# Inducing-point attention and a gated feed-forward on one core: gates and side work share a ring of double PSUM banks, one running maximum a batch, stage 2 by pairs

## The chip, the cores and the metric

The kernel runs on one core of a Trainium2 chip. The metric is the time of one execution in microseconds (us) of device time; less is better. PE is TensorE (matmuls), DVE VectorE, ACT ScalarE, POOL GpSimd, SP the SyncE that issues most DMAs.

## The reference

Two layers, one behind the other. The attention has 4 batches of 12416 tokens with 128 channels and 32 inducing points:

```python
def mab(q, kv):
    s = scale * (q @ kv.transpose(0, 2, 1))
    s = s - s.max(-1, keepdims=True)
    a = np.exp(s)
    a /= a.sum(-1, keepdims=True) + 1e-09
    return a @ kv
h = mab(I, x)
return mab(x, h).astype(np.float32)
```

Its output (49664 tokens of 128) goes through the feed-forward, with 1536 hidden units:

```python
gate = 1.0 / (1.0 + np.exp(-(x @ w_gate)))
val = x @ w_val
return (gate * val @ w_out).astype(np.float32)
```

## The kernel before

**Stages.** A batch has 97 chunks of 128 tokens: six groups of 16 chunks and one lone chunk. Stage 1 (`mab(I, x)`) makes scores of the 32 inducing points against a group, takes a maximum of the group (`s1_max`, L202, DVE, from PSUM), an exponential with it as bias (`s1_exp`, L215, ACT), turns the weights round (by a transposing DMA, L239, or on PE for the lone chunk), and sums weights times x (`s1_sum_pe`, L250). `plan_combine` brings the groups of a batch, each with a maximum of its own, to one (POOL, L370 and the tree behind it), divides, and multiplies h into the gate and value weights: `hw` holds h times the weights, 32 rows for each. So a hidden unit of the feed-forward is a product over 32 inducing points, not over 128 channels. Stage 2 (`mab(x, h)`) makes the 32 scores of each token (`s2_score`, L418), copies them out of PSUM (`s2_take`, L455, ACT), finds the maximum of each token and takes it away on POOL (`s2_lower_pool`, L457), exponential on ACT (L479), sum, reciprocal and normalised weights on POOL (`s2_sum_pool`, `s2_inverse_pool`, `s2_spread`), and a transposing DMA on SP's queue (`s2_turn_dma`). The result is `a2`.

**The feed-forward** runs over 97 blocks of 512 tokens. A block has 12 hidden tiles of 128 units, worked in steps of two tiles and one tile in turn. For a step t PE fills a value bank and a gate bank (`hidden_mm`, L791, K = 32, in row groups of their own), ACT takes the gate's tanh (L809), and DVE makes u = (tanh + 1) x value (L818). PE projects u with `w_out` into `acc` (`project`, L847: four matmuls a tile), and ACT copies a finished block out, halved (L865).

**PSUM** has eight banks: gates two (double tiles) and one (single), values the same (`g2`, `g1`, `v2`, `v1`, each one buffer), `acc` one, and `m` one for all side work, that is all of stages 1 and 2 beside the feed-forward.

**Order.** Each engine runs its queue in the order in which the program names its instructions. In step t: value fill of t, gate fill of t + 2, product of t, tanh of t + 2, then side work due in this slot (`plan`, `at`; a slot is two steps), then up to three or four tiles of projection. A double product waits for the gate fill of t + 2. Stages 1 of the next batch and 2 of this and the next are laid into slots by hand, at the end of the function (L872 to L904).

**Start.** Stage 1 of batch 0, stage 2 of its first group, and the weights come before the first block, with the same functions and an order of their own; maxima of the last groups are joined at the end (`join_min`).

Of the kernel before, what the change touches and what calls it, by code (L numbers as in the profile page):

```python
# [17 lines left out]
P = 128  # L18
# [7 lines left out]
def kernel(  # L26
# [29 lines left out]
    s1p = ctx.enter_context(tc.tile_pool(name="s1p", bufs=4))  # L56
# [12 lines left out]


    xn, xT = {}, {}

    def x_load(b, s, first=0):
        c0, n = groups[s]
        if s == 0:
            c0, n = 0, n + NLO
        if b not in xn:
            xn[b] = xnp.tile([P, NCH, C], F16, tag="xn", name=f"xn_{b}")
        cuts = [c0, c0 + first, c0 + n] if first else [c0, c0 + n]
        for c, e in zip(cuts, cuts[1:]):  # L80
            nc.gpsimd.dma_start(xn[b][:, c:e, :], xv[b, :, c:e, :])
# [5 lines left out]
    def x_transpose_dma(b, s):  # L87
        c0, n = groups[s]
        xT_tile(b)
        nc.sync.dma_start(  # L90
            xT[b][:, c0 : c0 + n, :],
            xn[b][:, c0 : c0 + n, :].rearrange("p j c -> p (j c)"),
            transpose=True,
        )
# [38 lines left out]
    one1 = const.tile([1, 1], F32, tag="one1")  # L133
    nc.vector.memset(one1[:], 1.0)
    tiny = const.tile([P, 1], F32, tag="tiny")
    nc.vector.memset(tiny[:], TINY)
    minus1 = const.tile([P, GC + NLO], F32, tag="minus1")
# [9 lines left out]
    nm1s = [const.tile([P, NS], F32, name=f"nm1_{q}", tag=f"nm1_{q}") for q in range(2)]  # L147
    l1s = const.tile([P, NS], F32, name="l1_0", tag="l1_0")
    hsts = [const.tile([P, NS, C + 1], F32, name=f"hst_{q}", tag=f"hst_{q}") for q in range(2)]
    nc.vector.memset(l1s[:], 0.0)  # L150
    for q in range(2):
        nc.vector.memset(nm1s[q][:], NEG)
        nc.vector.memset(hsts[q][:, at_col[NG], :], 0.0)

    indT = const.tile([P, m], F16, tag="indT")
    indT_ps = ps.tile([P, m], F32, tag="m", name="indT_ps")
    nc.tensor.matmul(indT_ps[:], ind32[:], identf[0:m, 0:m], start=True, stop=True)
    nc.vector.tensor_scalar_mul(out=indT[:], in0=indT_ps[:], scalar1=SCALE)
# [3 lines left out]
    summed = [0] * B  # L162
    def s1_sum(b, s, a1, tag):
        hp = ps.tile([P, C + 1], F32, tag=tag, name="hp_ps")
        s1_sum_pe(b, s, a1, hp, 0, 4)
        return s1_sum_keep(b, s, hp)

    plan = {}

    def at(slot, make, late=False):  # L170
        plan.setdefault((slot, late), []).append(make)


    def s1_col(b, s):
        p = at_col[s]
        if b == 0 and p >= EARLY:
            return nml, l1l, slice(1 + p - EARLY, 2 + p - EARLY)
        return nm1s[b % 2], None if b else l1s, slice(p, p + 1)
# [6 lines left out]
    def s1_score_pe(b, s, tag):  # L185
        c0, n = groups[s]
        ng, w, R = s1_dims(s)
        s1 = ps.tile([P, 512], F32, tag=tag, name="s1_ps")
        for g in range(ng):
            nc.tensor.matmul(  # L190
                s1[32 * g : 32 * g + 32, 0 : w * P],
# [4 lines left out]
            )  # L196
        return s1

    def s1_max(b, s, s1):
        ng, w, R = s1_dims(s)  # L200
        nm, _, col = s1_col(b, s)
# [4 lines left out]
    def s1_score(b, s, tag):  # L206
        s1 = s1_score_pe(b, s, tag)
        s1_max(b, s, s1)
        return s1

    def s1_exp(b, s, s1):
        ng, w, R = s1_dims(s)
        nm, l1, col = s1_col(b, s)
        a1T = s1p.tile([P, 512], F16, tag="a1T")
        nc.scalar.activation(  # L215
            out=a1T[0:R, 0 : w * P],
# [3 lines left out]
            **({} if b else dict(accum_out=l1[0:R, col])),  # L220
# [3 lines left out]
    def s1_turn_pe(b, s, a1T, tag="m"):  # L224
        ng, w, R = s1_dims(s)
        aT = ps.tile([P, 4, P], F16, tag=tag, name="aT_ps")
        for k in range(w):
            nc.tensor.transpose(aT[:, k, 0:R], a1T[0:R, ts(k, P)], ident[0:R, 0:R])  # L228
        return aT

    def s1_turn_copy(s, aT):
        ng, w, R = s1_dims(s)
        a1 = s1p.tile([P, 4, P], F16, tag="a1")
# [3 lines left out]
    def s1_turn_dma(b, s, a1T):  # L237
        a1 = s1p.tile([P, 4, P], F16, tag="a1")
        nc.sync.dma_start(a1[:], a1T[:], transpose=True)  # L239
        return a1  # L240

    def s1_sum_pe(b, s, a1, hp, k0, k1):
        c0, n = groups[s]
        ng, w, R = s1_dims(s)
        for k in range(k0, min(k1, w)):
            for cols, src in ((slice(0, C), None), (slice(C, C + 1), ones16[:])):
                for g in range(ng):
                    if b == 0 and src is not None:
                        continue
                    nc.tensor.matmul(  # L250
                        hp[32 * g : 32 * g + 32, cols],
                        a1[:, k, 32 * g : 32 * g + 32],
                        xn[b][:, c0 + g * w + k, :] if src is None else src,
                        start=(k == 0 and src is None),
                        stop=(k == w - 1),
                        skip_group_check=True,
                    )

    def s1_sum_keep(b, s, hp):
        ng, w, R = s1_dims(s)  # L260
        width = C + 1 if b else C
        summed[b] += 1
        if b == 0 and at_col[s] > EARLY:
            return hp[:, 0:C]
# [696 lines left out]
```

## Time and profile before

| | |
|---|---|
| time, median of 3 runs | 730.15 us (730.0 to 739.06) |
| span of the profiled execution, first to last instruction | 728.4 us |
| TensorE clock granted, mean | 0.988 |
| first product of the feed-forward | 33 us into the span |
| products (L818) | 388 of 1024 elements, 387 of 512, 2 of 256 |

The time of the profiled execution is not listed by itself. Busy time is the union of an engine's records; where neighbouring records overlap, a group's count times its mean is more than its busy time. A group's line gives: line of the kernel, engine, operation, output and inputs by the program's names with their shapes, count, busy time in us, mean duration in ns, then idle time of the engine just before them and what ended it. "DVE busy in stages": from 100 to 700 us it is 99.9% or more of every 100 us, ScalarE 95 to 97%, TensorE 90 to 91%, GpSimd 43 to 74%. The DMA engines are 89% busy from 40 to 100 us, then half or less. A timeline line gives the start in us, the length in us of what was merged, engine, line, operation, and how many.

### The profile page before, as it was taken

What the parts mean: (1) busy time and instruction counts of PE and PEld (TensorE: products, weight loads), DVE (VectorE), ACT (ScalarE), POOL (GpSimd) and SP (SyncE); (2) the same over time, 40 slices, a digit from 0 to 9 for tenths busy, and PEclk for the clock granted to TensorE, in tenths of its full rate; (3) what the DMA queues carried; (4) which work ended last, traced back from release to release, by engine and by line L of the source; (5) the groups of instructions that cost most, each with busy time, mean ns of one, the idle gap of its engine ahead of it and who ended that gap; (6) DMA issues with size and microseconds to landing.
All of it is one profiled execution on the core that took longest, in us unless ns stands there. A gap on an engine that the chain in (4) does not pass through costs nothing.

```text
span 728.4 us, 21430 instructions
## 1 busy us (share of the span) xinstructions
PE 645.6 (89%) x8406; PEld 392.7 (54%) x8406; DVE 706.0 (97%) x873; ACT 675.1 (93%) x1011; POOL 419.0 (58%) x702
## 2 busy tenths in 40 slices
PE   6798888999998989999988989999999899898887
PEld 4354555555555555555555555555555555555555
DVE  3898999999999999999999999999999999999998
ACT  4688999999999999999999999999999999999996
POOL 3553836688764548488757275387865665636200
PEclk9799999999999999999999999999999999999999
DMA  9899565143547372326169530320222122121211
GB/s 172 145 161 201 98 118 103 45 103 90 91 100 168 68 147 67 81 60 133 48 114 162 103 90 31 87 69 36 75 60 74 45 60 68 43 67 45 60 45 45
DMA packets 117749, 65.19 MB, mean 89 GB/s; under 512 B 101360, under 2 KB 102032, under 8 KB 117648
## 3 DMA queue, kind: packets, MB, share of 16 engines
q1 hardware_dynamic: 111936, 49.81, 30.4%
q0 software_dynamic: 5440, 13.90, 11.2%
q8 instruction: 65, 1.06, 0.6%
q14 instruction: 36, 0.29, 0.2%
q10 hardware_dynamic: 272, 0.13, 0.1%
HBM read 27.80 MB, written 25.43 MB: 73 GB/s over the span
## 4 chain that ended last, share of the span: by engine, by line
DVE 55%; issue 24%; PE 11%; ACT 5%; DMA 3%; DVEq 1%; POOL 0%; ACTq 0%; POOLq 0%
DVE u L818 53%; ACT t L809 5%; PE acc_ps L847 4%; PE v_ps L791 3%; DMA a<-a1T 2%; DVE nm L202 2%; PE xt_ps L612 1%; DVEq L818 1%; DMA xn<-in_x_dram 1%; PE hp_ps L250 1%; PE s_ps L190 0%; PE g_ps L791 0%; ACT a1T L215 0%; PE s_ps L418 0%; PE aT_ps L228 0%
## 5 line engine op out<-in xcount | busy, mean ns | idle before, releaser
L818 DVE SCALAR_TENSOR_TENSOR u<-t,v_ps 128x1024 f16<-128x1024 f16 (+1 forms) x777 | 675.5, 939 | 5.1 <-PE g_ps L791 4.7
L809 ACT ACTIVATE t<-g_ps 128x1024 f16<-128x1024 f32 (+1 forms) x776 | 593.7, 819 | 33.3 <-ACT t L809 17.5
L791 PE MATMUL v_ps<-a2r,hwt 32*128 32x512 f16 (+1 forms) x1188 | 294.4, 372 | 65.6 <-DVE u L818 64.6
L847 PE MATMUL acc_ps<-wo,u 128*128 128x128 f16 x4656 | 329.6, 221 | 0.0
L847 PEld LDWEIGHTS <-u 128*128 128x128 f16 x4656 | 262.8, 98 | 88.8 <-issue 87.8
L791 PE MATMUL g_ps<-a2r,hwt 32*128 32x512 f16 (+1 forms) x1188 | 297.5, 378 | 0.0
L791 PEld LDWEIGHTS <-hwt 32*128 32x128 f16 x2400 | 91.1, 91 | 197.7 <-issue 153.4
L487 POOL TENSOR_TENSOR sum<-e 128x256 f32<-128x256 f16 (+1 forms) x23 | 15.4, 671 | 148.2 <-ACT e L479 144.2
L533 POOL TENSOR_TENSOR a2n<-e,rs 128x2048 f16<-128x2048 f16 (+2 forms) x24 | 86.2, 3593 | 6.7 <-PE g_ps L791 2.8
L511 POOL TENSOR_TENSOR near<-sme,minus 128x16 f32<-128x16 f32 (+1 forms) x22 | 65.2, 2963 | 1.8
L865 ACT ACTIVATE o<-acc_ps 128x512 f32<-128x512 f32 x96 | 58.3, 607 | 0.0
L466 POOL TENSOR_SCALAR rise<-rise 128x256 f32<-128x256 f32 (+6 forms) x110 | 51.1, 464 | 9.7
L465 POOL TENSOR_TENSOR rise<-sc 128x256 f32<-128x256 f32 (+1 forms) x22 | 16.2, 738 | 38.9 <-ACT sc L455 38.7
L467 POOL TENSOR_TENSOR top<-top,rise 128x128 f32<-128x128 f32 (+3 forms) x88 | 28.3, 321 | 7.3
L487 POOL TENSOR_TENSOR sum<-sum 128x128 f32<-128x128 f32 (+3 forms) x92 | 28.3, 307 | 7.2
L465 POOL TENSOR_TENSOR rise<-top 128x128 f32<-128x128 f32 (+3 forms) x88 | 27.1, 308 | 6.9
L470 POOL TENSOR_TENSOR sc<-sc,top 128x512 f32<-128x512 f32 (+1 forms) x22 | 23.9, 1084 | 1.7
L418 PEld LDWEIGHTS <-xT 128*128 128x128 f16 x388 | 13.4, 97 | 12.2 <-issue 12.2
L418 PE MATMUL s_ps<-hT,xT 128*128 128x32 f16 x388 | 18.2, 179 | 0.3 <-DVE hT L315 0.3
L467 POOL TENSOR_TENSOR top<-sc,rise 128x256 f32<-128x256 f32 (+1 forms) x22 | 16.3, 740 | 1.8
L250 PE MATMUL hp_ps<-xn,a 128*32 128x128 f16 x388 | 14.2, 225 | 2.9 <-DMA a<-a1T 2.6
L215 ACT ACTIVATE a1T<-s_ps,nm 128x512 f16<-128x512 f32 (+1 forms) x24 | 15.1, 628 | 1.7 <-DVE nm L202 1.7
(118 smaller groups left out, 235.9 us busy)
## 6 DMA issues: line engine op xcount, KB each, us to landing
out_dram<-o SPq DMA_DIRECT2D x96, 256.0 KB, 2.3
xn<-in_x_dram POOLq DMA_DIRECT2D x19, 512.0 KB, 8.1
xn<-in_x_dram POOLq DMA_DIRECT2D x4, 544.0 KB, 6.3
a2r<-a2n SPq DMA_TRANSPOSE x29, 4.4
xn<-in_x_dram POOLq DMA_DIRECT2D x1, 384.0 KB, 14.6
wg<-in_moe_w_gate_dram POOLq DMA_DIRECT2D x1, 384.0 KB, 4.4
wv<-in_moe_w_val_dram POOLq DMA_DIRECT2D x1, 384.0 KB, 5.4
wo<-in_moe_w_out_dram POOLq DMA_DIRECT2D x1, 384.0 KB, 5.5
```

Source lines behind the costliest of these rows:

```text
L418: nc.tensor.matmul(s2[:, j, :], xT[b][:, c + j, :], hT16[b][:], start=(j == 0), stop=whole and j == j1 - 1, skip_group_check=True,)
L465: nc.gpsimd.tensor_tensor(out=r, in0=far, in1=near, op=ALU.subtract)
L466: nc.gpsimd.tensor_scalar_max(out=r, in0=r, scalar1=0.0)
L467: nc.gpsimd.tensor_tensor(out=top[:, 0:n, 0:w], in0=near, in1=r, op=ALU.add)
L487: nc.gpsimd.tensor_tensor(out=d[:, 0:n, :], in0=src[:, :, 0:w], in1=src[:, :, w : 2 * w], op=ALU.add)
L511: nc.gpsimd.tensor_tensor(out=near[:, 0:n], in0=sme[:, 0:n], in1=minus1[:, 0:n], op=ALU.pow)
L533: eng.tensor_tensor(out=a2n[:, 0:n, :, :], in0=e.unsqueeze(2).to_broadcast((P, n, 4, m)), in1=rs.unsqueeze(2).unsqueeze(3).to_broadcast((P ...
L791: st[what + "end"] = nc.tensor.matmul(pt[:, k, col : col + nb * P], hw[b][r : r + 32, j // 2, :], a2r[r : r + 32, o : o + nb, :].rearrange ...
L809: st["tanh"] = nc.scalar.activation(out=st["t"][:], in_=st["g"][:], func=AF.Tanh, scale=0.5)
L818: u = nc.vector.scalar_tensor_tensor(out=st["u"][:, :, c:e], in0=st["t"][:, :, c:e], scalar=1.0, in1=st["v"][:, :, c:e], op0=ALU.add, op1= ...
L847: nc.tensor.matmul(acc[0][(i // 2) % len(acc[0])][:, i, :], st["u"][:, k, ts(i, P)], wo16[:, j, :], start=(j == 0 and i in ((0, 2) if len( ...
L865: nc.scalar.mul(out=o32[:], in_=acc[0][0][:], mul=0.5)
```

## The change

PSUM's split is new. The gates get a ring of two double tiles (four banks, tag `g`, two buffers), and all side work takes its PSUM from the same ring, read by ACT alone. Values keep their double and their single bank, `acc` its own.

A block is now two halves of six hidden tiles. A half has three gates of two tiles each, whose tanh goes into one tile of six (two buffers), and four products, of 2, 1, 2 and 1 tiles. The loop's step is a product: value fill of the next product; side fill if the half has one (steps 0 and 1); at steps 1 to 3 a gate fill of the next half; the product; the side's read by ACT behind the last side fill; the tanh of that gate; planned work; projection.

```diff
-    for t in range(NST):
-        product(t)
-        gate(t + 2)
-        if t % 2 == 0:
-            beside(t // 2, False)
-        else:
-            beside(t // 2, True)
-            project(t - 1, t, 3 if waiting(t - 1) <= 3 else 4)
+    rest = 0
+    for half in range(NH):
+        fills, take = parts.pop(half, ([], None))
+        for k in range(4):
+            p = 4 * half + k
+            value_fill(p + 1)
+            if k < len(fills):
+                fills[k]()
+            if k > 0:
+                gate_fill(half + 1, k - 1)
+            product(p)
+            if fills and k == len(fills) - 1:
+                take()
+            if k > 0:
+                gate(half + 1, k - 1)
+            for make in plan.pop((half, k), ()):
+                make()
+            if rest:
+                rest -= 1
+            else:
+                room = (1 if fills else 2, 1, 3, 2)[k]
+                if project(p, room):
+                    rest = 1
```

```diff
+    CUTS = [(0, 2), (2, 1), (3, 2), (5, 1)]
...
+    def gate_fill(half, i):
+        if half < NH:
+            gates[(half, i)] = ring_tile("g_ps")
+            hidden_mm(gates[(half, i)], half, 2 * i, 2, "g")
...
+    def value_fill(p):
+        if p < NP:
+            j0, cnt = CUTS[p % 4]
+            values[p] = ps.tile([P, cnt, 512], F32, tag=f"v{cnt}", name="v_ps")
+            hidden_mm(values[p], p // 4, j0, cnt, "v")
```

Stage 1 of the batches 1 to 3 copies its scores to SBUF two groups at a time (one ring tile, one ACT copy 1024 wide), and POOL keeps a running maximum over the groups, element by element. DVE makes one maximum of it for the batch, and the exponentials, two groups at a time, all take the same bias; so the groups' sums add up without weights.

```diff
+    def raise_to(top, other, rise):
+        nc.gpsimd.tensor_tensor(out=rise, in0=other, in1=top[0], op=ALU.subtract)
+        nc.gpsimd.tensor_scalar_max(out=rise, in0=rise, scalar1=0.0)
+        nc.gpsimd.tensor_tensor(out=top[1], in0=top[0], in1=rise, op=ALU.add)
...
+        def score_take(i):
+            nc.scalar.copy(out=st["sc"][:, 2 * i : 2 * i + 2, :], in_=st["ps"][:])
+            for s in range(2 * i, 2 * i + 2):
+                if s:
+                    low = st["sc"][:, 0, :] if s == 1 else st["M"][:]
+                    raise_to((low, st["M"][:]), st["sc"][:, s, :], st["rise"][:])
...
+        def least():
+            ml = bp.tile([P, 1], F32, tag="ml")
+            nc.vector.tensor_reduce(out=ml[:], in_=st["M"][:], axis=AX.X, op=ALU.max, negate=True)
+            st["top"] = join_min(bp, ml)
+        at(o + lower, 3, least)
```

The sums come out of three ring tiles (two groups each), the last with the lone chunk; h, and the weights times h, pass through ring tiles too. The lone chunk is turned by a DMA as well.

Stage 2 takes its groups by pairs: two score halves (each a ring tile and an ACT copy 512 or 544 wide), then one lowering, one exponential, one sum, one reciprocal on POOL (in batch 0 on DVE), and two spreads, on tiles of up to 33 chunks. Only the second group of batch 0 goes alone, with its maximum on DVE from SBUF.

There is one x buffer where there were two: x of a batch lies in `xn_all`, the loads of the batch after next come behind the sums. The start takes its PSUM from the first two ring tiles.

```diff
-    xnp = ctx.enter_context(tc.tile_pool(name="xnp", bufs=2))
+    xnp = ctx.enter_context(tc.tile_pool(name="xnp", bufs=1))
...
-    up = ctx.enter_context(tc.tile_pool(name="up", bufs=6))
-    tp = ctx.enter_context(tc.tile_pool(name="tp", bufs=4))
+    up = ctx.enter_context(tc.tile_pool(name="up", bufs=5))
+    tp = ctx.enter_context(tc.tile_pool(name="tp", bufs=2))
```

The due times, in halves (`o` is the first half of a batch's blocks, 48 a batch; a pair is half and step):

```diff
+            plan_stage2(0, [1], False, [0], (1, 2), (2, 3), [(4, 0)], o)
+            plan_stage2(0, [2, 3], False, [3, 5], (8, 0), (9, 2), [(11, 0), (12, 0)], o)
+            plan_stage2(0, [4, 5], True, [17, 19], (23, 2), (25, 1), [(27, 0), (28, 0)], o)
+        else:
+            plan_stage2(b, [2, 3], False, [1, 3], (7, 2), None, [(12, 0), (13, 2)], o)
+            plan_stage2(b, [4, 5], True, [17, 19], (23, 2), None, [(28, 0), (29, 1)], o)
...
+            score=[9, 11, 15],
+            lone_at=13,
+            lower=18,
+            weigh=[(20, 1), (22, 0), (24, 0)],
+            turn=[(21, 1), (23, 0), (25, 0)],
+            sums=[25, 27, 29],
+            total=31,
+            take=32,
+            fill=37,
+        )
+        plan_stage2(b + 1, [0, 1], False, [33, 35], (39, 2), None, [(44, 0), (45, 2)], o)
...
+                at(o + 30 + 2 * g, 2, lambda b=b, g=g: x_load(b + 2, g))
+                at(o + 36 + 2 * g, 2, lambda b=b, g=g: x_transpose_dma(b + 2, g))
```

In `plan_stage2` the arguments are the groups, whether the lone chunk is among them, the halves of the scores, the slot of the exponential (with POOL's sum, and reciprocal and spread if no slot is given for these), that of the reciprocal and spread, and those of the transposing DMAs.

More of the change, by code (lines that the diff above doesn't have):

```diff
@@ L298, with side, at @@
+    parts, plan = {}, {}
+    def side(half, fills, take):
+        assert half not in parts
+        parts[half] = (fills, take)
+    def at(half, step, make):
+        plan.setdefault((half, step), []).append(make)
     hT16 = {}
@@ L595, in plan_stage2 @@
[L595 to L605 removed]
+            if inverse is None:
+                spread(s2_inverse_pool(n, st["sme"]))
@@ L608, in x_turn, with turn @@
+        at(o + weigh[0], weigh[1], exp)
+        if inverse is not None:
+            at(o + inverse[0], inverse[1], lambda: spread(s2_inverse(n, st["sme"])))
+        def turn(i):
+            s2_turn_dma(b, groups[gs[i]][0], GC, st["a2n"], "a2r", i * GC)
+            if far and i == len(gs) - 1:
+                s2_turn_dma(b, 0, NLO, st["a2n"], "a2l", 2 * GC)
+        for i in range(len(gs)):
+            at(o + turns[i][0], turns[i][1], lambda i=i: turn(i))
     def x_turn(b, c0, n, tag):
         xT_tile(b)
-        xt = ps.tile([P, 2, 8, P], F16, tag=tag, name="xt_ps")
+        xt = bank(tag, [P, 2, 8, P], F16, "xt_ps")
```

711 lines of the change are left out of this document (380 added, 331 removed).

## The prediction

> **What bounds the kernel now.** I read the page's busy times and its chain, then the groups by shape, then the chain and the timeline of a quiet stretch near 600 us, then GpSimd's groups. First the page:
>
> ```profile
> PE 645.6 (89%) x8406; PEld 392.7 (54%) x8406; DVE 706.0 (97%) x873; ACT 675.1 (93%) x1011; POOL 419.0 (58%) x702
> DVE 55%; issue 24%; PE 11%; ACT 5%; DMA 3%; DVEq 1%; POOL 0%; ACTq 0%; POOLq 0%
> ```
>
> DVE is the fullest engine and carries the chain, ScalarE and TensorE are close behind. By shape:
>
> ```profile
> L818 DVE SCALAR_TENSOR_TENSOR u<-t,v_ps 128x1024 f16<-128x1024 f16 x388 | 468.5, 1208 | 3.4 <-PE g_ps L791 3.0
> L809 ACT ACTIVATE t<-g_ps 128x1024 f16<-128x1024 f32 x388 | 400.6, 1032 | 31.8 <-ACT t L809 17.5 <-PE g_ps L791 6.4 <-PE v_ps L791 1.3
> L818 DVE SCALAR_TENSOR_TENSOR u<-t,v_ps 128x512 f16<-128x512 f16 x387 | 260.4, 673 | 1.7 <-PE g_ps L791 1.7
> L202 DVE TENSOR_REDUCE nm<-s_ps 128x1 f32<-128x512 f32 x20 | 13.6, 678 | 0.9 <-PE s_ps L190 0.9
> L455 ACT COPY sc<-s_ps 128x512 f32<-128x512 f32 x22 | 13.1, 593 | 0.0
> ```
>
> The products wait only 5.1 us in all. How far apart they start, the chain between 600 and 605 us says:
>
> ```profile
> 600.64 1.16 DVE u L818 x2
> ...
> 602.37 1.16 DVE u L818 x2
> ...
> 604.10 1.16 DVE u L818 x2
> ```
>
> One double and one single product take 1.73 us, although their records sum to 1.88: neighbours overlap by 0.08. So a double advances DVE by 1.13 and a single by 0.60. With 388 pairs the products need 671 us, and nothing in the change makes them fewer or narrower. The rest of the 728.4 us span is start (first product at 33 us), end, DVE's other work and 5 us of waiting. The timeline of the same stretch gives the other engines' beat:
>
> ```profile
> 599.52 1.51 ACT L809 ACTIVATE t<-g_ps 128x1024 f16<-128x1024 f32 x2 [0.22 <-ACT t L809]
> 599.63 0.37 PE L791 MATMUL v_ps<-a2r,hwt 32*128 32x512 f16 x1 [0.20 <-DVE u L818]
> 599.95 0.84 PE L847 MATMUL acc_ps<-wo,u 128*128 128x128 f16 x12
> 600.76 0.39 PE L791 MATMUL v_ps<-a2r,hwt 32*128 32x512 f16 x2
> 600.92 0.60 ACT L865 ACTIVATE o<-acc_ps 128x512 f32<-128x512 f32 x1
> 601.36 0.37 PE L791 MATMUL v_ps<-a2r,hwt 32*128 32x512 f16 x1 [0.20 <-DVE u L818]
> ```
>
> A 512-wide ScalarE operation advances it by 0.48 (600.92 to 601.40, the next tanh), a 1024-wide one by 0.92 (599.52 to 600.92 less 0.48). A fill starts 0.05 after the product that frees its bank (single ends 601.31, fill 601.36); a projection starts 0.32 after the fills ahead of it. Twelve projection matmuls and the turn to the next fill take 0.78 (423.60 to 424.38 in another stretch), so eight take 0.55. A fill's end is 0.06 ahead of its product and 0.09 ahead of its tanh (606.36 to 606.42, 606.37 to 606.45). The double value fill is thus ready at 601.15 for a product at 601.23: TensorE has some 0.1 us to spare where it is tightest.
>
> **Part by part.** *DVE's side work.* The later batches' stage 1 loses 18 wide maxima (0.60 apart, 10.8) and three narrow ones (0.27 a record, 0.6), three 32-wide copies (L234) and gains three maxima of the running maximum (1.8). Net, with small reciprocals, -9.7 us. All of it lies on DVE's path, so it is a gain in full.
>
> *Gates 1024 wide.* A half block (six hidden tiles, products at steps 0 to 3, 3.46 us) had 2 x 0.92 + 2 x 0.48 = 2.80 of tanh and gets 3 x 0.92 = 2.76. ScalarE has 3.46 - 2.76 - 0.24 (half an `o`) = 0.46 us free a half; the 0.04 is off the path and worth nothing.
> By the Trainium skill (Perfetto Trace Analysis, Optimizing Scalar/DVE Operations) grouping into larger operations raises throughput if the engine is saturated; ScalarE's 93% looks so, but the record overlap says it is not. If it were, that rule would give 194 x 0.04 = 8 us, an estimate from the rows above.
>
> *The ring.* This is the step I weigh most. Side work takes ring places: five score halves in batch 0, four in each later batch, two for each coming batch's first pair, so 23 stage 2 halves, and per later batch 3 scores, 3 sums, one weight fill, and two short ones. All but the short ones fill at steps 0 and 1 and are read by ScalarE at step 1, ahead of the next half's first tanh. I count from the start of the double product at step 0. It ends at 1.20; the double value fill runs at 1.26, the side part's second half at 1.58. Eight stage 2 score matmuls take 0.37 (417.77 in the trace): done 1.95, read by ScalarE 2.04 to 2.64 (593 ns). The next half's second gate fill needs this ring place, and TensorE stands in front of it, at step 2, until 2.69; it would have been there at 1.86. Behind it are queued two projected tiles (eight matmuls: that is what the rooms 1, 1, 3, 2 and the rest after each block leave in these halves) and then the double value fill for the next half's first product. So: 2.69 + 0.32 + 0.55 = 3.56, filled 3.95, product at 4.01 instead of 3.46. That is 0.55 us of DVE, gone, since a product cannot catch up; generally the end of the side read less 2.09. In the same way:
> - stage 1 scores, 4 matmuls 0.40, a read 1024 wide. No row has it: between one 512-wide copy (0.59) and two (1.19); I take 1.02, a copy plus the tanh rows' step. End 3.09, stall 1.00 (bounds 0.57 to 1.17).
> - weight fill, 768 wide, read 0.81: stall 0.79.
> - sums, 0.54 of matmuls (four chunks at 407.35's pace), read 0.29: stall 0.57.
> Sum: 23 x 0.55 + 9 x 1.00 + 3 x 0.79 + 9 x 0.57 = 29.2 us. Bounds: nothing, if TensorE's wait is covered; 12.5, if only ScalarE's order counts (below); 35, if the first parts at step 0 delay the fill of step 1 by another 0.1.
>
> *Wide exponentials.* Nine stage 1 and ten stage 2 ones, each 0.92 put between tanhs. In a quiet half the third tanh ends at 4.59 and its first product starts at 5.19, cover 0.55. Cost 0.35 each, 6.7 us; bounds 0 (they replace 18 + 22 narrow ones that are hidden now) and 0.7 where two follow each other.
>
> *GpSimd.* It gets the running maximum (five raises of three 512-wide operations a batch) and pairs instead of single groups:
>
> ```profile
> L511 POOL TENSOR_TENSOR near<-sme,minus 128x16 f32<-128x16 f32 x18 | 52.8, 2935 | 1.5
> L466 POOL TENSOR_SCALAR rise<-rise 128x256 f32<-128x256 f32 x18 | 15.5, 859 | 1.6
> L467 POOL TENSOR_TENSOR top<-sc,rise 128x256 f32<-128x256 f32 x18 | 13.2, 734 | 1.5
> L470 POOL TENSOR_TENSOR sc<-sc,top 128x512 f32<-128x512 f32 x18 | 19.3, 1074 | 1.4
> ```
>
> No row is 512 wide in this form: from 128 to 256 elements L467 grows from 452 to 734, so 1.30 at 512 (bounds 0.73 and 1.47), L466 about 1.53. A raise is 4.4 with gaps, a pair's lowering 13.0 (8.6 for one group now, 591.2 to 599.8), its sum 3.6, reciprocal 6.6, spread 7.3. In batch 0 the pair's last score is read by 2.64 of half 5, its exponential stands at the front of half 8, 9.2 us later: ScalarE waits, 3.8 us come through to DVE. In the two middle batches the maximum (DVE, step 3 of half 18) waits for raises queued behind a pair's sum and spread, about 1.1 us each. Together 6 us; bounds 0 and 12.
>
> *At no cost.* One x buffer: the loads for the batch after next go behind the sums, and their transposes six halves (20.8 us) later, cover 8.1 us of landing; without it TensorE waits for x, as it now does for `a<-a1T` (2.6 us). Those waits should go, as sums come 13 us after the transpose is issued. SP gets fewer transposes; output stores wait behind them with four buffers. I credit the 5.1 us that products wait now.
>
> Sum: 728.4 - 9.7 - 5.1 + 29.2 + 6.7 + 6 = 755.5 span. The profiled execution's time is not listed; the median is 730.15, 1.75 above its span, so 757 us.
>
> **Rivals.**
> *The ring is covered: not slower.* If the side read were done before 2.09 (or the projections did not stand between the gate fill and the value fill), no product waits, and exponentials and GpSimd stay hidden as now: 713.6 span, 715 us; with some waits up to 728. For: today's side reads cost nearly nothing. Against: today's have a bank of their own, and no gate waits for them. The grouping rule of the skill's page above also points here. Chance 0.18.
> *ScalarE's order alone.* TensorE's wait costs nothing but the first tanh comes behind the read: stage 2 2.04 + 0.48 + 1.03 + 0.06 - 3.46 = 0.15, scores 0.62, fills 0.45, sums 0.2, together 12.5. Span 738.5, 740 us. Chance 0.22.
> *GpSimd decides.* If its 512-wide operations are at the upper bound, lowering and raises are a tenth longer, every batch's exponential and maximum wait 3 to 8 us: 775 to 785 us. For: its margins are under 1 us. Against: it is only 58% busy. Chance 0.15.
>
> **How the numbers follow.** Forecast (745 to 770 us) 0.45. The range 720 to 785 leaves out the lower part of the first rival and the end of the last. A measurement here tells about 2%: under 715.5 is faster, 0.07, since only the first rival at its best goes there; 715.5 to 744.8 is the rest of it, the second and a little more: 0.35; slower 0.58.
>
> **What would show it.** After: pair of products still 1.73 in quiet halves; DVE waiting some 0.5 to 1 us in each side half, put down to PE `v_ps`; PE `g_ps` waiting for ScalarE copies; DVE without L202 in the main stretch; one long ScalarE wait for GpSimd in half 8. If DVE stays 99% busy to the end, the ring step is wrong and the time is near 715.

## The result, and the profile after

The changed kernel takes 812.0 us (median of 4 runs, 809.0 to 822.9), the kernel before 730.1 (median of 4): a ratio of 1.106, interval 1.097 to 1.115. The forecast was 757, with 785 as the upper end. The profiled execution took 809.0 us, its span is 807.1. Below, "clock" is the granted TensorE clock; where an experiment spent long stretches at half of it, its whole time is no measure of the edit, and halves at full clock are compared.

The busy times and the chain by engine on the page of the changed kernel, then its products by shape:

```profile
PE 724.0 (90%) x8185; PEld 429.8 (53%) x8185; DVE 718.8 (89%) x848; ACT 668.9 (83%) x791; POOL 406.3 (50%) x456
...
PE 47%; DVE 37%; ACT 9%; issue 4%; POOL 1%; DMA 1%; DVEq 0%; POOLq 0%; ACTq 0%
```

```profile
L949 DVE SCALAR_TENSOR_TENSOR u<-t,v_ps 128x1024 f16<-128x1024 f16 x388 | 473.6, 1221 | 50.7 <-PE g_ps L909 33.8 <-issue 8.2 <-PE v_ps L909 4.2
...
L949 DVE SCALAR_TENSOR_TENSOR u<-t,v_ps 128x512 f16<-128x512 f16 x387 | 263.8, 682 | 12.5 <-PE g_ps L909 9.8 <-PE v_ps L909 1.5
```

DVE went from 97% busy to 89%, although the products are as long as they were: they now wait 63.2 us, where they waited 5.1. TensorE carries 47% of the chain, where it carried 11%. ScalarE and GpSimd fell too (93 to 83%, 58 to 50%): neither became the bound.

To see where the waits lie, take on VectorE the time from each product's start to the start of the instruction behind it, and subtract the 1.13 us of a double or the 0.60 of a single that the prediction read off a quiet stretch. What is left is the time lost at that product. A quiet half is one without side work. Sorted by what the half has beside it (all from the two traces, in us):

| | before | after | the prediction's term |
|---|---|---|---|
| first product starts | 33.1 | 40.4 | unchanged |
| products at full pace | 671.3 | 671.3 | unchanged |
| other VectorE work, with the end | 16.7 | 8.7 | -9.7 |
| quiet halves (107) | | 8.0 | 0 |
| stage 2 score halves (21) | | 12.1, that is 0.575 each | 0.55 each |
| stage 1 score halves (8) | | 9.1, 1.14 each | 1.00 each |
| weight fill halves (3) | | 2.4, 0.79 each | 0.79 each |
| sum halves (9), and the halves behind them | | 26.5, 2.94 each, and 4.4 | 0.57 each, 5.1 |
| halves 20 to 24, and 8 and 40 | | 9.0 and 2.5 | 6.7 |
| halves 8 to 10 of batch 0 | | 6.1 | 3.8 |
| first four halves, lone chunk and total, last block | | 3.7, 1.2, 1.2 | 0 |
| time lost at products: all rows from the quiet halves on | 6.8 | 86.2 | |

The first three rows and the last add up to 727.9 and 806.6, each 0.5 short of its span: there VectorE's closing instructions lie. (One stage 1 score half is counted in batch 0's halves 8 to 10, two stage 2 ones in the first four.)

The first place to look is a quiet half, where nothing was expected. The chain between 600 and 605 us:

```profile
601.47 1.23 DVE u L949
602.70 0.04 issue
602.74 0.39 PE v_ps L909 x2
603.13 0.05 PE g_ps L909 x2
603.18 1.77 DVE u L949 x3
```

The chain passes from VectorE to TensorE and back at the half's last step. VectorE's wait ends 0.05 after the value and gate fills have (603.13 to 603.18), and the half is 3.53 us long, not 3.46. In the trace two things stand ahead of such a product on VectorE, a wait for TensorE's fill by itself and then the product with its wait for the tanh. The half's first product starts 0.107 after its value fill has ended, where a double product of the kernel before mostly started 0.082 after, at the full pace behind the product ahead of it.

The chain over a stage 2 score half that begins at 305.14:

```profile
306.44 0.36 PE v_ps L909 x2
306.81 0.30 PE s_ps L512 x8
307.11 0.32 PE g_ps L909 x2
307.43 0.33 PE acc_ps L974 x4
307.75 0.32 PE v_ps L909
308.07 0.10 PE g_ps L909 x2
308.17 0.55 PE acc_ps L974 x8
308.72 0.32 PE v_ps L909 x2
309.04 0.07 PE g_ps L909 x2
309.15 1.23 DVE u L949
```

The next half's product comes at 309.15, 4.01 us after the first, as predicted to the hundredth. But the chain has no wait on it. TensorE is at work from end to end: the wait for the side read, 0.83 us in the prediction (1.86 to 2.69), is 0.09 here (the second `g_ps` runs 0.09 behind its `v_ps`). In its place stand other pieces of TensorE's own work, among them a gate fill by itself, 0.32 at 307.11. Before, TensorE's matmuls of a like half were these:

```profile
417.45 0.39 PE L791 MATMUL v_ps<-a2r,hwt 32*128 32x512 f16 x2
417.45 0.39 PE L791 MATMUL g_ps<-a2r,hwt 32*128 32x512 f16 x2
417.77 0.37 PE L418 MATMUL s_ps<-hT,xT 128*128 128x32 f16 x8
```

Value and gate fill start together, on different rows of the array, and the next work follows 0.32 later: a gate fill beside a value fill costs nothing, one by itself 0.32. The sums, last, in TensorE's timeline after and then before (`hp_ps<-ones` are the ones matmuls, which add up the weights):

```profile
540.02 0.24 PE L421 MATMUL hp_ps<-xn,a 128*32 128x128 f16 x4
540.19 0.18 PE L429 MATMUL hp_ps<-ones,a 128*128 128x1 f16 x1
540.30 0.24 PE L421 MATMUL hp_ps<-xn,a 128*32 128x128 f16 x4
540.47 0.18 PE L429 MATMUL hp_ps<-ones,a 128*128 128x1 f16 x1
540.58 0.24 PE L421 MATMUL hp_ps<-xn,a 128*32 128x128 f16 x4
```

```profile
407.35 0.24 PE L250 MATMUL hp_ps<-xn,a 128*32 128x128 f16 x4
407.41 0.18 PE L250 MATMUL hp_ps<-ones,a 128*32 128x1 f16 x4
407.44 0.23 PE L250 MATMUL hp_ps<-xn,a 128*32 128x128 f16 x4
407.50 0.18 PE L250 MATMUL hp_ps<-ones,a 128*32 128x1 f16 x4
407.62 0.37 PE L791 MATMUL v_ps<-a2r,hwt 32*128 32x512 f16 x1
```

The diff made one ones matmul of 128 columns out of four of 32. A chunk is 0.28 us (540.02 to 540.30) where it was 0.135 (0.27 for two), and that at full clock, which is 1.00 from 539.3 to 543.4. Behind it the clock falls: here are the windows of a sum half and of a quiet one (columns: length, busy time of PE, PEld, the weight loads, DVE, ACT and POOL, then PEclk, the granted clock, the DMA engines' busy share, and GB/s):

```profile
539.30:545.70 6.40, 6.40 (x78) 3.70 (x77) 3.75 (x5) 3.44 (x6) 3.64 (x1) 0.82 0.43 83
600.00:603.50 3.50, 2.97 (x35) 1.69 (x32) 3.50 (x5) 3.42 (x5) 3.50 (x1) 1.00 0.00 0
```

Half speed covers 71 us of the span after, 19 before. The Trainium skill (TensorE: Matmul & The Clock Gate, Part 1) has the clock halve after an idle window of some 3.4 us. The stretches here last 3.4 us or a multiple of it (6.8, 20.5), but TensorE's records, whose ends are modelled, fill 6.40 of the 6.40 us shown, and all of the 4.10 us ahead of the stretch that begins at 543.4, so an idle window doesn't explain this one.

### The profile page after: what moved, and what is told of

The parts are those of the page before. It is cut to its first block, busy times and chain, and to the rows that moved or that the text cites. A ratio compares the mean times of both kernels' runs of the same rounds, so it can differ in the third digit from the quotient of the medians.

```text
span 807.1 us, 19763 instructions
## 1 busy us (share of the span) xinstructions
PE 724.0 (90%) x8185; PEld 429.8 (53%) x8185; DVE 718.8 (89%) x848; ACT 668.9 (83%) x791; POOL 406.3 (50%) x456
## 4 chain that ended last, share of the span: by engine, by line
PE 47%; DVE 37%; ACT 9%; issue 4%; POOL 1%; DMA 1%; DVEq 0%; POOLq 0%; ACTq 0%
DVE u L949 36%; PE v_ps L909 18%; PE acc_ps L974 18%; ACT t L929 5%; PE g_ps L909 4%; PE s_ps L512 2%; PE hp_ps L421 2%; ACT e L571 1%; ACT sc L360 1%; ACT o L992 1%; PE s_ps L200 1%; PE hp_ps L429 1%; PE near_ps L719 1%; ACT a1T L393 1%; DMA xn<-in_x_dram 1%
## 5 line engine op out<-in xcount | busy, mean ns | idle before, releaser
L949 DVE SCALAR_TENSOR_TENSOR u<-t,v_ps 128x1024 f16<-128x1024 f16 (+1 forms) x777 | 695.5, 950 | 63.2 <-PE g_ps L909 43.6
L929 ACT ACTIVATE t<-g_ps 128x1024 f16<-128x1024 f32 x582 | 558.3, 1028 | 42.1 <-ACT t L929 25.9
L974 PE MATMUL acc_ps<-wo,u 128*128 128x128 f16 x4656 | 391.3, 226 | 10.2 <-ACT o L992 8.9
L909 PE MATMUL g_ps<-a2r,hwt 32*128 32x512 f16 (+1 forms) x1188 | 229.0, 386 | 1.3
L909 PEld LDWEIGHTS <-hwt 32*128 32x128 f16 x2400 | 111.4, 91 | 163.3 <-issue 82.8
L293 POOL TENSOR_SCALAR rise<-rise 128x512 f32<-128x512 f32 (+10 forms) x73 | 63.5, 870 | 6.4
L667 ACT COPY sc<-s_ps 128x512 f32<-128x512 f32 (+1 forms) x23 | 13.6, 590 | 22.0 <-PE s_ps L512 16.7
L562 POOL TENSOR_TENSOR sc<-sc,top 128x1024 f32<-128x1024 f32 (+1 forms) x11 | 21.8, 1985 | 0.9
L579 POOL TENSOR_TENSOR sum<-sum 128x128 f32<-128x128 f32 (+8 forms) x48 | 20.2, 420 | 3.8
L294 POOL TENSOR_TENSOR top<-top,rise 128x256 f32<-128x256 f32 (+7 forms) x44 | 20.2, 459 | 3.7
L292 POOL TENSOR_TENSOR rise<-top 128x256 f32<-128x256 f32 (+7 forms) x44 | 19.0, 431 | 3.4
```

The lines of the kernel that those rows point to most:

```text
L292: nc.gpsimd.tensor_tensor(out=rise, in0=other, in1=top[0], op=ALU.subtract)
L293: nc.gpsimd.tensor_scalar_max(out=rise, in0=rise, scalar1=0.0)
L562: nc.gpsimd.tensor_tensor(out=sc[:, 0:n, :], in0=sc[:, 0:n, :], in1=top.to_broadcast((P, n, m)), op=ALU.subtract,)
L579: nc.gpsimd.tensor_tensor(out=d[:, 0:n, 0:w], in0=src[:, 0:n, 0:w], in1=src[:, 0:n, w : 2 * w], op=ALU.add)
L909: nc.tensor.matmul(pt[:, k, col : col + nb * P], hw[b][r : r + 32, j // 2, :], a2r[r : r + 32, o : o + nb, :].rearrange("p j t -> p (j t)" ...
L929: nc.scalar.activation(out=t16[half][:, 2 * i : 2 * i + 2, :], in_=gates.pop((half, i))[:], func=AF.Tanh, scale=0.5,)
```

## The experiments

The theory at first: four separate costs, each with a cause of its own (the ones column, the wait by itself, the start, the ring). The rival was that they are one: TensorE being late anywhere.

**Ones column.** Four matmuls of 32 columns again (`g` runs over 0 to 3):

```diff
                 nc.tensor.matmul(
-                    hp[:, C : C + 1],
-                    a1,
+                    hp[32 * g : 32 * g + 32, C : C + 1],
+                    a1[:, 32 * g : 32 * g + 32],
                     ones16[:],
```

> The matmul against the column of ones in the stage 1 sums takes 32 columns of weights four times again, as in the kernel before, instead of 128 once. Theory: the change of tile shape, 32 columns to 128 and back, is what makes a chunk of the sums take 0.28 us on TensorE where it took 0.14, so a side part takes 1.11 instead of 0.55; with it undone the nine sums halves fall from 6.1-7.0 us to 4.2-4.8 and the span from 807 to about 785. Rival: these halves are long because the granted clock halves in them, which one-column matmuls bring about in either shape; then they stay above 5.5 us and the span above 800.

Measured: 791.5 us (ratio 1.085, 1.081 to 1.090), 16 us of span less. A sum half loses 0.89 instead of 2.94, the half behind it 0.07 instead of 0.49. Its matmuls:

```profile
528.53 0.24 PE L421 MATMUL hp_ps<-xn,a 128*32 128x128 f16 x4
528.60 0.18 PE L430 MATMUL hp_ps<-ones,a 128*32 128x1 f16 x4
528.63 0.23 PE L421 MATMUL hp_ps<-xn,a 128*32 128x128 f16 x4
```

A chunk takes 0.10 here, and the half speed stretches in halves 24 to 30 go from ten to two. Of the edits tried by themselves it is worth most. It undoes shape and clock together; what the shape does alone, two sum halves say that kept the full clock with the ones matmul of 128 columns: half 27 of batch 1 loses 2.06 us in the run with the start on banks of its own and 2.10 in the one with the projection first, against 0.75 here. So some 1.3 of the 2.05 us is the shape, and the rest lies with half speed.

**Projection first.** In a half with side work, at step 2, the projected tiles go ahead of the gate fill that waits for a ring place (excerpt; the usual place of the projection is then skipped):

```diff
+            first = bool(fills) and k == 2
+            if first:
+                assert not rest and not project(p, 3)
             if k > 0:
                 gate_fill(half + 1, k - 1)
```

> In a half with side work the two tiles projected at step 2 go ahead of the gate fill that waits for the side's read, not behind it. Theory of the prediction (what is queued behind that wait makes the next value fill late): a stage 2 half falls from 4.01 to about 3.65-3.75 us, a stage 1 score half from 4.57 to 4.1-4.25, the weight fill half from 4.25 to 3.95, the span by 12 to 18 us. Rival, ScalarE's order alone (the first tanh comes late behind the side's read): nothing moves, less than 4 us.

Measured: 845.3 us, with 173 us at half speed (clock 0.90), so only halves at full clock count. There stage 2 score halves take 3.95 to 4.06 (4.01 without the edit), the half behind 0.1 more: nothing gained. Stage 1 score halves take 4.10 to 4.24 (4.57), with 0.27 more in the half behind; fills 4.11 (4.25). So for stage 2 the wait alone was not what held the half, as the chain above says; for the wider stage 1 read it was, though most of the gain is given back behind it.

**One wait.** The first product of a half waits for the gate fill two on, which itself waits for that product's tanh, and so for one event in place of two (excerpt):

```diff
+        if p % 4 == 0 and h >= 2:
+            tc.declare_no_dep(u.ins, tanh[(h, 0)].ins, reason="the gate fill two on waits for it")
+            tc.add_manual_dep(u.ins, gend[(h, 2)].ins.name, AFTER, reason="tanh, gate fill, product")
```

> The first double product of a half waits for the end of the gate fill two places on in the ring (which itself waits for that tanh) in place of the tanh and the value fill, as double products did in the kernel before. Theory: the quiet half of 3.53 instead of 3.46 us comes from a second semaphore that DVE waits for ahead of a double product; with one of the two undone the step from single to double falls from 0.635 to 0.60, a quiet half to 3.49, and the span by 6 to 9 us. Rival: the fill itself is later than before, and a single wait changes nothing, under 2 us.

Measured: 807.4 and 825.1 us, the profiled one with 135 us at half speed. At full clock the quiet half is 3.49 instead of 3.53, the loss at its last step 0.00 instead of 0.04, and the product starts 0.070 after its value fill instead of 0.107: the second wait costs 0.04 us a half.

**The start on banks of its own.** A PSUM pool for the start, closed before the ring is made, as the kernel before had it (excerpt):

```diff
-    ps = ctx.enter_context(tc.tile_pool(name="ps", bufs=1, space=bass.MemoryType.PSUM))
+    early = ExitStack()
+    ps = early.enter_context(tc.tile_pool(name="ps0", bufs=1, space=bass.MemoryType.PSUM))
...
+    early.close()
+    ps = ctx.enter_context(tc.tile_pool(name="ps", bufs=1, space=bass.MemoryType.PSUM))
```

> The start has its own PSUM tiles of one and two banks again, given back before the ring is made. Theory: in the start two uses that share one double tile wait for each other although they lie in different banks; with tiles of their own the first product comes at 33 to 35 us instead of 40.4, and the span falls by 5 to 8 us. Rival: the granted clock (half speed from 18 to 21 and 25 to 28 us) makes the start late; then the first product stays behind 38 us.

Measured: 806.2 us. The first product starts at 33.3 instead of 40.4, 7.2 us earlier, though half speed lies there as well (25.5 to 39.2): it is the two uses that share one double tile and wait for each other. (The three other runs with the shared tiles start at 37.7 to 40.5.) The span falls by 2.6 only, since half speed lasts 78 us and the sums lose 29.0 where they lost 26.5.

**The three together.**

> Three steps undone together: 32-column matmuls for the column of ones, one wait for the first double product of a half, PSUM tiles of its own for the start. If the three costs are separate they add up: sums halves near 4.4 us, quiet halves 3.49, first product near 33 us, span 807 - 20 - 7.5 - 7 = 770 to 777, where the clock is not at half for long. If they hide each other, 780 or more.

Measured: 781.6 us (778.3 and 784.9). First product 32.8, quiet half 3.49, sum halves 1.5 each with the half speed ones among them. The gains of the three hold together: the span of the run of 778.3 us, 776.5 at a clock of 0.973, lies in the range, and that of the profiled one, 783.1 with 64 us at half speed, above it. Stage 2 score halves stay at 3.98, stage 1 ones at 4.58.

**Gate first.** On top of these, at step 1 the next half's first gate fill goes ahead of the side's second part, so that it runs beside the value fill:

```diff
+            ahead = k == 1 and len(fills) == 2
+            if ahead:
+                gate_fill(half + 1, 0)
             if k < len(fills):
                 fills[k]()
-            if k > 0:
+            if k > 0 and not ahead:
                 gate_fill(half + 1, k - 1)
```

> As the kernel with three steps undone, and at step 1 of a half with two side fills the gate fill goes ahead of the side's second fill, so that it runs beside the value fill again (they use other rows of the array). Theory: the half with side work is long because TensorE has too much to do in it (the side fill, and a gate fill that runs alone), not because of the wait for the ring; 0.3 us less work makes a stage 2 half 3.98 to about 3.70, a score half 4.55 to 4.2-4.3, sums and fill halves 0.2-0.3 shorter, the span 9 to 14 us less than without. Rival: the wait for the side's read decides; then the halves stay within 0.1 us, since the read ends no earlier.

Measured: 775.3 us (clock 0.975). Sum halves at full clock fall from 4.20 to 4.05, but stage 2 score halves stay at 3.99 and stage 1 ones at 4.59. I took this for a second limit, the wait for the side's read.

**Store first.** At step 0 the projection and the copy of `o` go ahead of the planned work, so that exponentials do not stand in front of `o`; built on gate first:

```diff
-            for make in plan.pop((half, k), ()):
-                make()
+            if k:
+                for make in plan.pop((half, k), ()):
+                    make()
...
+            for make in plan.pop((half, k), ()):
+                make()
```

> As the kernel before it in this list, and at step 0 the projection with its block's copy out of PSUM (ScalarE) comes ahead of the planned work, exponentials among it. Theory: at halves 8 and 24 of a batch the copy stood behind an exponential, and the next block's first projection, which needs the one accumulator bank, held TensorE up ahead of the value fill (PE acc_ps waits 8.9 us for ACT o in all); with the copy ahead half 24 falls from 5.0-5.2 to 4.0 us, half 8 of batch 0 by about 1 us, the span by 4 to 6 us. Rival: the exponential itself on ScalarE is what delays; then less than 1.5 us.

Measured: 781.8 us (777.2 and 786.5), span 775.4 against 774.5: no gain in the whole. At its last step half 8 of batch 0 loses 3.17 instead of 4.75. Half 24 at full clock loses 1.39 there with and without the edit (batch 0 had lost 2.10 without it, but with half speed inside), and half 22 loses 0.27 more in each of three batches. So the order of `o` helps only where the exponential waits for GpSimd.

**Both limits undone**: gate first and projection first, on the version with the three.

> Built on the version with the ones column in 32 columns, one wait ahead of a product, the start on banks of its own and the gate fill ahead of the side's second half; added: at step 2 of a half with side work the tile of the projection goes ahead of the gate fill that has to wait for a place in the ring. That version left the halves with a stage 2 score at 3.99 us, and the step alone, in the kernel as changed, left them at 3.96 to 4.06. Theory: the wait for a place in the ring and TensorE's own lateness are two limits of nearly equal size, so only both edits together set the halves free: stage 2 score halves at 3.6 to 3.7 us, stage 1 score halves from 4.59 to 4.1 to 4.2, some 7 us and 3 us in all, span 762 to 767 at the same clock. Rival 1: a third thing, ScalarE's own order (the read and two tanhs ahead of the next gates), holds the halves at 3.9 to 4.0, span 772 to 777. Rival 2: the projection ahead takes from the value fill what it gives the gate fill, and the wait only moves to the half behind it (stage 2 halves 3.6, the next ones 3.9), span again 772 to 777.

Measured: 781.9 us (1.074, 1.063 to 1.084); profiled span 776.6. Stage 2 halves 3.99, stage 1 halves 4.59 to 4.62, unchanged within 0.03, so a third thing held them. The chain over such a half, which began at 228.50, shows it:

```profile
230.50 0.02 ACT sc L650
230.52 0.46 issue
230.98 1.04 ACT t L916
232.02 0.04 issue
232.06 0.41 PE g_ps L894 x2
232.46 0.02 issue
232.49 1.23 DVE u L936
```

The value fill had ended at 3.42 from the half's start and the tanh at 3.51, but the product stood until the gate fill two on, which follows the tanh, was over at 3.95. That is the one wait of an earlier edit. It saves 0.04 in quiet halves, where the fill is done early, and costs 0.4 in these. It had hidden what the two edits did.

**The wait left as it was behind side work**, on gate first alone and on both (`busy` holds the halves with side work):

```diff
-        if p % 4 == 0 and h >= 2:
+        if p % 4 == 0 and h >= 2 and h - 1 not in busy:
```

> The version with the gate fill ahead of the side's second half, with one edit: behind a half with side work the first product of the next half waits for its tanh again, and not for the gate fill two on. In the trace of the version with the projection ahead as well, that gate fill ran from 3.56 to 3.95 us after the half's first product (it waits for a tanh that ends at 3.51) and the next product began at 3.99, while its value fill had ended at 3.42: so the one wait that saves 0.05 us in quiet halves costs 0.4 us here, and it hid what the edits to TensorE's order did. Theory: two limits of nearly equal size stand ahead of that product, TensorE's own order (value fill ends at 3.90 in this version) and the ring's chain (side read, tanh at 3.51). This version undoes only the second: stage 2 halves at 3.95 to 3.98 us instead of 3.99, stage 1 halves 4.5 to 4.6, span 773 to 776 at the same clock. Rival: only the wait put in by the earlier edit held these halves, 3.6 to 3.7 us here already, span 762 to 766.

Measured: 782.9 us (two runs, 1.064, 1.053 to 1.075; clock 0.960). Stage 2 halves 4.01, stage 1 halves 4.61 to 4.64: gate first alone frees nothing, and the rival falls.

> The same edit of the wait, on the version with the gate fill ahead of the side's second half and the projection ahead at step 2. Theory of two limits: both are gone here (value fill ends at 3.42, tanh at 3.51), so the next product starts 3.56 to 3.65 us after the half's first one in stage 2 halves (21 of them, 0.34 to 0.43 each: 7 to 9 us) and at 4.03 to 4.15 in stage 1 halves (8 of them, some 0.5 each: 4 us): span 762 to 766 at a clock of 0.975. Rival 1 (ScalarE's own order or the value fill of the half behind takes it back): 3.6 us here and 3.8 to 3.9 in the half that follows, span 773 to 777. Rival 2 (something not seen yet): still 3.99.

Measured: 788.1 us (775.1 to 796.5), 77 us of the profiled execution at half speed, mostly around the sums; the whole time says nothing of the edit. At full clock the stage 2 halves are 3.54 to 3.62 (but for one of 3.67 and one of 3.88), the fills 3.82 instead of 4.27 and the stage 1 halves 4.14 to 4.17, as the theory of two limits has it. The half behind each takes 3.76 instead of 3.49, so rival 1 is half right: of some 0.41 us gained in a stage 2 half 0.27 is given back, and 21 of them are worth 3 us, not 8. These are TensorE's matmuls of such a half, which began at 230.68:

```profile
231.95 0.39 PE L894 MATMUL v_ps<-a2r,hwt 32*128 32x512 f16 x2
231.95 0.39 PE L894 MATMUL g_ps<-a2r,hwt 32*128 32x512 f16 x2
...
233.67 0.39 PE L894 MATMUL g_ps<-a2r,hwt 32*128 32x512 f16 x2
233.71 0.39 PE L894 MATMUL v_ps<-a2r,hwt 32*128 32x512 f16 x2
234.24 0.39 PE L894 MATMUL g_ps<-a2r,hwt 32*128 32x512 f16 x2
```

Two of the three gate fills run beside a value fill again, and the value fill starts 3.03 after the half's first product, where it started at 3.51 in the changed kernel (308.65 after 305.14).

**One maximum a batch alone**, in the kernel before: banks, gates and stage 2 as they were, stage 1 with GpSimd's running maximum, one x buffer and later exponentials (excerpt).

```diff
+            nc.scalar.copy(out=st["sc"][:, s, :], in_=st["s1"][:])
+            if s:
+                low = st["sc"][:, 0, :] if s == 1 else st["M"][:]
+                raise_to(low, st["sc"][:, s, :], st["rise"][:], st["M"][:])
```

> One part of the change alone, in the kernel before: PSUM, gates, steps and single groups in stage 2 as before, but stage 1 of batches 1 to 3 copies its scores to SBUF (ScalarE, 512 wide), GpSimd keeps the running maximum, DVE makes one maximum a batch, exponentials by pairs, one x buffer. Theory: DVE is the bound, and 18 wide maxima less by three new ones take 9.4 us off its path; ScalarE gets 18 copies of 0.48 us and has room: 719 to 723 us against 729. Rival: ScalarE has no room or GpSimd (138 of 166 us a batch) comes late: 728 to 745 us.

Measured: 773.8 us (1.061, 1.038 to 1.084), 85 us at half speed. In the view of waits:

```profile
ACT a1Tp L311 <- POOL top L442: 21.6, 3, 7.2
```

The exponential waits 7.2 us in each batch for the joined maximum, which is queued on GpSimd behind a stage 2 block's sum and spread. That is the wait that the prediction placed in half 18 of the changed kernel, and didn't find there; it lies here. Moving slots (scores and maxima earlier, exponentials and the third block later):

> The kernel before with one change alone, the single maximum of stage 1 in a batch (one set of scores kept, GpSimd raises the maximum, the exponentials later), with banks, gates and stage 2 as before; against the first trial of this, four scores are taken in the first gap of GpSimd, the third stage 2 block's exponential goes three slots later, and stage 1's exponentials two slots later, so that the joined maximum stands ahead of the stage 2 block on GpSimd. In the first trial the exponential waited 7.2 us a batch for that maximum. Theory: VectorE sets the time, and with room on GpSimd what the prediction took for VectorE's side work, 9.7 us, comes out of the span, less up to 3 us in the halves where a wait is left: 719 to 724 us, ahead of the kernel before by 1 to 1.5%. Rival: GpSimd is too full for it wherever the slots lie, one of its consumers waits 3 us or more in each batch, and half speed stretches follow: 735 to 760.

Measured: 764.7 us (1.050, 1.040 to 1.060). That wait is gone, another has come, by the view of waits:

```profile
DVE u L867 <- PE g_ps L840: 40.9, 26, 9.0
...
PE g_ps L840 <- DMA a2r<-a2n: 27.0, 4, 8.5
```

GpSimd now lowered the next block between the third block's sum and its spread, so its transpose was late by 9 us a batch. With the joined maximum between that block's sum and spread, the lowering behind both, and each wide exponential cut in two of 512 (excerpt):

```diff
-            lower=o + 37,
-            weigh=[(o + 41, o + 42), (o + 43, o + 44), (o + 46, o + 47)],
+            lower=o + 36,
+            weigh=[(o + 39, o + 41), (o + 41, o + 43), (o + 44, o + 46)],
```

> The kernel before with the one maximum a batch alone, against the last trial of it: that one lost 9.0 us a batch at a stage 2 transfer, because GpSimd lowered the next block between the third block's sum and its spread. Here the joined maximum stands between that block's sum and spread and the lowering behind both, stage 2's slots are as in the kernel before, and each of stage 1's wide exponentials is cut into two of 512 in neighbouring slots (0.6 us lost at each of two wide ones). Theory: VectorE sets the time, and what is left of 762 is 762 less 27, less some 3 to 5 for the half speed stretch behind each wait, less 2 to 4 for the exponentials: 722 to 732, and the median between 724 and 734. Rival: ScalarE, which has 0.3 us to spare in four slots and gets seven copies more a batch, sets the time in the stage 1 stretch: 738 to 750.

Measured: 733.6 us (median of 10), ratio 0.998, 0.994 to 1.001, against a kernel before that took 736.7 on that chip (median of 13, 728.1 to 738.8): no gain. The profiled spans are 731.6 and 728.4, so the theory's range is met at its upper edge, but not by the gain that it claimed. VectorE's other work is 7.0 us, 9.7 less than the kernel before has, and the products lose 20.1 us, 13.3 more. In the stretch where stage 1 is done, first this kernel's window, then the same one of the kernel before (columns as above):

```profile
251.00:308.00 57.00, 51.28 (x705) 31.51 (x702) 53.71 (x62) 54.95 (x84) 42.10 (x70) 0.97 0.27 67
```

```profile
255.00:312.00 57.00, 51.73 (x741) 31.81 (x740) 56.98 (x71) 54.84 (x86) 33.17 (x67) 1.00 0.43 94
```

VectorE has 53.7 us of 57 to do where it had 57.0; ScalarE is as full as it was, near 55 of 57, with the score copies that the one maximum needs in place of work done straight from PSUM. What VectorE saves becomes waiting, in what would be halves 12 to 24, at the 0.25 to 1.35 us that single steps lose. That they lose it to copies and exponentials among ScalarE's tanhs is read from the rows; no run made ScalarE's work less. Why the waits exceed the saving by 3.6 us was not separated; two half speed stretches of 3.4 us lie there as well.

## Right and wrong, step by step

- *DVE's side work*, -9.7, "a gain in full": the size is right (-8.0 in the change, where reciprocals and the end took some of it; -9.7 in the last version above). "In full" is wrong. In the change products wait anyway, and done alone it comes back as waits, by the rows above behind a ScalarE that is as full as VectorE.
- *Gates 1024 wide*, worth nothing: not tested by itself. But that a gate fill in 1024 comes less often beside a value fill, and costs TensorE 0.32 by itself, was in no step.
- *The ring*: stage 2 0.55 (0.575), fill 0.79 (0.79), stage 1 1.00 (1.14): the sizes are right. The mechanism is half right. In a stage 2 half TensorE's wait for the place was 0.09, not 0.83, since it reached that point 0.7 later: a gate fill by itself, a projected tile and a single value fill stood ahead of it. The wait and TensorE's own order are two limits of nearly one size; undone one at a time they gave nothing, together 0.4 a half, of which 0.27 went into the next one. In stage 1 halves the mechanism is right: the projection first alone brought 4.10 to 4.24, and both edits no more, 4.14 to 4.17.
- *The ring, sums*, 0.57 each "at 407.35's pace": the step that failed most. I priced the old matmuls; the diff has one of 128 columns among those of 32, at 0.28 a chunk instead of 0.135, and the clock, for which the sum has no term, fell on top. A sum half lost 2.94 instead of 0.57: 31 us with the halves behind, against 5. Four matmuls of 32 columns gave back 2.05 a sum half, some 1.3 of it by the shape at full clock. What made the clock fall stays open.
- *Start unchanged*: 7.4 us late. The start takes its PSUM from two ring tiles, as the section on the change says; that two uses in one tile wait for each other was not weighed.
- *Quiet half 3.46*: 3.53 measured, 8 us over 107 halves. The credit of 5.1 us for waits that should go had 8 us of new ones against it.
- *Wide exponentials*, 0.35 each, 6.7: halves 8 and 40 lose 0.35 each, as said; halves 20 to 24 lose 9.0. In half 24 of batch 2 two wide exponentials with one tanh between them, the lone one and `o` fill ScalarE from 523.87 to 527.56, ahead of the next tanh; that they are the cause is read from the trace, no run moved them apart.
- *GpSimd*: half 8 of batch 0 loses 4.7 (3.8 predicted), the waits of 1.1 in half 18 are not there. GpSimd does not decide in the change.
- Of "what would show it", the missing maxima and the wait in half 8 came (ScalarE 3.4 us for GpSimd). The fills of `g_ps` do not show long waits for ScalarE's copies: their idle time is 1.3 us in all. DVE's waits in side halves are put down to `g_ps` rather than `v_ps`, and the pair was not 1.73 throughout.
- In the rival *ScalarE's order alone* the terms add up to 12.2 and not to 12.5; its 738.5 is right.

By sum: the start 7.4, the sums 26, the quiet halves 8, the exponentials 5, the first halves 4 make 50 of the 51.6 us between the predicted span, 755.5, and the measured one; the rest is small terms of both signs.

## What to carry to other kernels

Price a moved or rewritten matmul by its own shape, not by the old one's pace; and where two fills share the array's rows, ask of a new order whether they still run side by side. When one edit shows no effect, look at the chain for a second limit of the same size before dropping the theory, and check that no earlier edit of your own is that limit. Work taken off the fullest engine is worth something only up to the next one's fill: here ScalarE stood at 55 of 57 us.

## What the runs showed of the hardware that was not expected

- A ones matmul over all 128 columns of the array, between matmuls over 32 of them, makes a chunk 0.28 us long at full clock instead of 0.10 to 0.135, although its own record is 0.18 us either way.
- A second event to wait for, ahead of a VectorE instruction, costs 0.04 us: the product starts 0.107 after its value fill with two, 0.070 with one.
- TensorE ran at half speed for up to 48 us at a stretch with no gap in its records (556.2 to 604.0 us in the run with the projection first: busy 47.80 of 47.80 us, clock 0.50). Half speed lay at the start, at the sums and behind long waits. What sets them off was not settled. Between the two runs of the version with one wait, 807.4 and 825.1 us, the mean clock was 0.953 and 0.919.
